# Giving out the steps of a windowed softmax one at a time, in a two-attention kernel whose instruction order comes from a planner

## The chip, the cores and the metric

One core of one Trainium2 chip. The metric is the device time of one execution in microseconds, median of several runs. Engines are named as the profile names them: PE (TensorE, matmuls; PEld are its weight loads), DVE (VectorE), ACT (ScalarE), POOL (GpSimd), SP (SyncE).

## The reference

Two attention layers over their own inputs, joined along the last axis. Both have 2048 positions, width 1024, 32 heads of 32. Layer A is dilated: each position sees 8 keys at distances 0, 2, ..., 14. Layer B sees the 256 latest keys.

```python
def _A_ref(x, wqkv, wo):
    qkv = (x @ wqkv) ...                      # q, k, v, each (1, 32, 2048, 32)
    off = jnp.arange(8) * 2
    idx = pos[:, None] - off[None, :]
    logits = jnp.einsum("bhsd,bhswd->bhsw", q, k[idx]) * Dh ** -0.5   # idx < 0 masked
    o = jnp.einsum("bhsw,bhswd->bhsd", softmax(logits), v[idx])
    return o.reshape(B, S, D) @ wo

def _B_ref(x, wqkv, wo):
    scores = q @ k.T * Dh ** -0.5             # masked to 0 <= i - j < 256
    return (softmax(scores) @ v).reshape(B, S, D) @ wo

return jnp.concatenate([A, B], axis=-1)
```

All is float32. The kernel reaches that precision on TensorE with pairs: a value is split into a high part and a rest, and three products of the pairs replace one.

## The kernel before, in words

**Units.** The work is cut into 8 units of 512 positions: units 0 to 3 are layer B, units 4 to 7 layer A. For layer A the even and the odd positions are laid out one after the other beforehand, so that a dilated window becomes a run of 8 neighbours. Each unit has 8 groups of 4 heads. For each group the projection of queries and keys is computed (`qk_items`, L616: 24 matmuls per weight tile), for several groups at once the values (`v_items`, L685), and one unit later the output projection (`o_items`, L749). A value part of four groups takes a new weight tile every 12 matmuls; such a part stands at the start of each unit.

**Splits.** Weights and inputs come in as float32 by loads that POOL issues (L182) into three buffers. `Stream.parts` splits them: a cast gives the high part, on ACT (L233) or DVE (L236), whichever the planner's books say is done sooner, and a subtraction on DVE gives the rest (L239), in pieces of 512 columns. `split_to` asks for a split; it is called where a matmul step is given out, mostly one tile ahead.

**Layer A's attention** (`window`). Scores of one group: 128 small matmuls into four banks (L822). Then, on a buffer `band` of 128 x 1152:
- four mask additions on DVE (L830);
- `top`: maximum (L840) and subtraction (L842) on DVE, then the exponential on ACT (L846);
- `total`: sum (L854), reciprocal (L856), product (L858) and two transposes of 32 x 32 blocks (L861, one for each half), all on DVE;
- `spread`, once for each half: eight copies on ACT (L870 and L873, four strips of two) that put the turned pieces in place along a diagonal of `wide`;
- values: small matmuls from `wide` and the values (L896), then the overlap of blocks is added and the result split (L994 to L1007) into `ot`, which the output projection reads.

**The planner.** The order on each engine is not the compiler's. While the program is built, an object `ck` of class `Clock` keeps books: `use` adds an operation's estimated time to an engine and returns when its result is seen, `defer(t, f)` calls `f` when the planned time of PE reaches `t`. The main loop picks, among four sequences (the projections `g`, scores `1`, values and second matmuls `2`, and `a`), the step that is ready first, gives out its matmuls, and calls what has fallen due in between. On the chip each engine then works through its instructions in the order in which they were given out; semaphores guard the data. Values are ready for the planner at `h["p"]`, which `spread` sets. Tables such as `PACE`, `HOLD` and `EDGES_V` shift these times by unit and group.

Of the kernel before, what the change touches and what calls it, by code (L numbers as in the profile page):

```python
# [9 lines left out]
AF = mybir.ActivationFunctionType  # L10
ALU = mybir.AluOpType
# [3 lines left out]
P = 128  # L15
# [19 lines left out]
PACE = ((0.4, 2.4, 0.1, 0.1, 0.4, -99, 4), (0.4, 1.8, 0.3, 0.1, 0.4, -99, 2), (0.1, 0.6, 0.3, 0.1, 0.0, -99, 2), (0.2, 2.4, 0.3, 0.1, 0.4, -99, 1), (6.0, 8.0, 0.5, 0.5, 1, 3), (2.0, 6.0, 1.5, 0.2, 1, 2), (4.0, 7.0, 0.5, 0.2, 1, 3), (4.0, 7.0, -0.5, 0.0, 1, 1))  # L35
# [7 lines left out]
HOLD = ((0, 1.2, 0, 0, 0, 0, 0, 0), (0, 0, 0, 0, 1.2, 0, 0, 0), (0.6, 0, 1.6, 0, 0, 0, 0, -0.4), (1.2, 0, 0, 0, 0, 0, 0, 1.2), (0, 0, 0, 0, 0, 0, 0, 0), (0, 0, 0, 0, 0, 0, 0, 0), (-0.4, 0, 0, 0, 0, 0, 0, 0), (0, 0, 0, 0, 0, 0, 0, 0))  # L43
# [7 lines left out]
class Clock:  # L51
# [6 lines left out]
    HOLD = dict(sp=0.63, act=0.35, pool=0.6)  # L58
    MOVE = dict(load=(2.12, 0.14), store=(0.64, 0.4), copy=(1.18, 0.56),
                halo_out=(0.4, 0.68), halo_in=(0.55, 0.6), halo_few=(0.28, 0.51),  # L60
                half=(1.0, 0.14), part=(0.33, 0.56))
# [96 lines left out]
class Stream:  # L158
# [68 lines left out]
    def parts(self, t, raw, t0, side):  # L227

        nc, ck = self.nc, self.ck
        n = raw.shape[1]  # L230
        bias = EARLY if side else self.light[self.split]
        if ck.ends("act", n / 1200 + 0.1, t0) <= ck.ends("dve", n / 1932 + 0.19, t0) + bias:
            nc.scalar.copy(t[:, 0, :], raw)  # L233
            r = ck.use("act", n / 1200 + 0.1, t0)
        else:
            nc.vector.tensor_copy(t[:, 0, :], raw)  # L236
            r = ck.use("dve", n / 1932 + 0.19, t0)
        for c in range(0, n, 512):
            nc.vector.tensor_tensor(t[:, 1, c:c + 512], raw[:, c:c + 512], t[:, 0, c:c + 512].bitcast(F32), op=ALU.subtract)  # L239
            end = ck.use("dve", 0.61, r, port=True)  # L240
        return end
# [19 lines left out]
def kernel(ctx, tc, xs, wqk, wv, wo, outs, units):  # L261


    nc = tc.nc
# [18 lines left out]
    ck = Clock()  # L283


    def parts_of(u):
        return VPARTS if len(V_AT[u]) == 3 else VPARTS_LATER
# [41 lines left out]
    for p in plan:  # L329
# [19 lines left out]
        else:  # L349
            u = p[1] - 1  # L350
# [8 lines left out]
    for key, i in where.items():  # L359
        u = min(key[1] + (key[0] == "o"), U - 1)  # L360
# [432 lines left out]
    def window(u, s):  # L793


        has_halo = units[u][3]
        buf = s % 2
        hg = u * NG + s
        vp, vc = vparts[parts_of(u)][s]
        v = vbufs[parts_of(u)][vp]  # L800

        def p96():
            return band[buf][:, :1536].rearrange("p (j b c) -> p j b c", j=4, b=4)

        def p16():
            return band[buf][:, :1536].rearrange("p (i c) -> p i c", c=96)[:, :, 24:]

        h = pairs[hg % 2] = {}

        def scores_ready():  # L810
            return latest(rs.empty(), done["stack"].get((u, s)),
                          latest(*[done["clear"].get(i) for i in range(2)]) if hg - 2 <= last_dense else
                          done["o"].get(hg - 2))

        def scores():
            qk = rows[hg]
            banks = [rs.take() for _ in range(4)]
            for b in range(4):
                for i in range(2):
                    for j in range(4):  # L820
                        c = P * b + 64 * i
                        nc.tensor.matmul(banks[j][0][64 * i:64 * i + 64, 72 * b:72 * b + 72],  # L822
                                         qk[32 * j:32 * j + 32, c:c + 64], qk[32 * j:32 * j + 32, S + c:S + c + 72],
                                         start=True, stop=True)
            seat_free(hg)

            def mask():
                m = cst["near"][:, 1:5] if has_halo else cst["near"][:, :4]
                for j in range(4):
                    nc.vector.tensor_tensor(p96()[:, j, :, 24:], banks[j][0][:, :288].rearrange("p (b c) -> p b c", b=4), m,  # L830
                                            op=ALU.add)
                    e = ck.use("dve", 0.37, ck.now)
                    rs.give(banks[j][1], e)
                ck.defer(e - 0.1, top)

            return mask

        def top():
            nm = small.tile([P, 16], F32, tag="nm", name="nm")
            nc.vector.tensor_reduce(nm, p16(), axis=mybir.AxisListType.X, op=ALU.max)  # L840
            ck.use("dve", 1.39, ck.now)
            nc.vector.tensor_tensor(p16(), p16(), nm[:, :, None].to_broadcast([P, 16, 72]), op=ALU.subtract)  # L842
            e = ck.use("dve", 1.39, ck.now, port=True)

            def expo():
                nc.scalar.activation(p16(), p16(), AF.Exp)  # L846
                e2 = ck.use("act", 1.07, e)
                ck.defer(e2 - 0.1, lambda: total(e2))

            ck.defer(e - 0.1, expo)  # L850

        def total(e):
            sm = small.tile([P, 16], F32, tag="sm", name="sm")
            nc.vector.tensor_reduce(sm, p16(), axis=mybir.AxisListType.X, op=ALU.add)  # L854
            ck.use("dve", 1.39, e)
            nc.vector.reciprocal(sm, sm)  # L856
            ck.use("dve", 0.285, ck.now)
            nc.vector.tensor_tensor(p16(), p16(), sm[:, :, None].to_broadcast([P, 16, 72]), op=ALU.mult)  # L858
            ck.use("dve", 1.39, ck.now, port=True)
            for i in range(2):  # L860
                nc.vector.transpose(turned[i], band[buf][:, 768 * i:768 * i + 768])  # L861
                e = ck.use("dve", 0.88, ck.now)
                ck.defer(e - 0.1, lambda i=i, e=e: spread(i, e))

        def spread(half, e):
            pieces = turned[half].rearrange("p (j b t c) -> p j b t c", j=2, b=4, t=3)
            diag = wide[buf][:, 2 * half:2 * half + 2].rearrange("p j (b c) -> p j b c", b=4)
            for i in range(4):
                r, c = 32 * i, 32 * i + 8
                nc.scalar.copy(diag[r:r + 32, :, :, c:c + 32], pieces[r:r + 32, :, :, 1 + i % 2, :])  # L870
                ck.use("act", 0.415, e)
                n, c = ((i - 1) * 32, c) if i else (96, 0)
                nc.scalar.copy(diag[n:n + 32, :, :, c:c + 8], pieces[r:r + 32, :, :, i % 2, :8])  # L873
                t = ck.use("act", 0.255, e)
            if half:
                h["p"] = t + PACE[u][3] + HOLD[u][s]

        def values_ready():
            if len(seats_x.free) < len(both):
                return None  # L880
            return latest(done["v"].get((u, vp)), *[x.get("p") for x in both], ro.when(),
                          rs.when() if alone else rs.empty())

        def values():
            own = ro if alone or s % 2 else rs
            h["o"], first_bank = own.take()
            h["o2"], bank = rs.take()
            halves = [h["o"], h["o2"]]
            blocks = [(-1, 1, 0, 8)] if has_halo else []
            blocks += [(b, i, P * b + 64 * i, min(72, S - P * b - 64 * i)) for b in range(4) for i in range(2)]  # L890
            seen = set()
            for b, i, q0, w in blocks:
                c = 136 * b + 8 + 64 * i if b >= 0 else 0
                r = slice(64 * i, 64 * i + 64)
                for j in range(4):
                    nc.tensor.matmul(halves[i][32 * j:32 * j + 32, q0:q0 + w],  # L896
                                     v[r, (4 * u + b) % 6, vc + 32 * j:vc + 32 * j + 32], wide[buf][r, j, c:c + w],
                                     start=(i, j) not in seen, stop=True, skip_group_check=True)
                    seen.add((i, j))

            return lambda: overlap(u, s, h, bank, own, first_bank, 0 if has_halo else 1)

        alone = s // 2 not in PAIRS[u]
        h["values"], both = values, [h] if alone else list(pairs)

        def two():
            ends = [x["values"]() for x in both]

            def after():
                for f in ends:  # L910
                    f()

            return after

        return [Item(scores_ready, scores, CW)], [Item(values_ready, two, C3 + len(both) * CP)] if alone or s % 2 else []
# [361 lines left out]
    while True:  # L1277
# [3 lines left out]
        for name, seq in seqs.items():  # L1281
# [3 lines left out]
            t = seq[pos[name]].ready()  # L1285
# [4 lines left out]
        if ck.later and (best is None or ck.later[0][0] < best[0]):  # L1290
            t = ck.later[0][0]
# [3 lines left out]
        t, name = best  # L1295
# [52 lines left out]
```

## Time and profile before

| | |
|---|---|
| median of 3 runs | 1779.6 us (1779.0 to 1781.2) |
| the profiled execution | 1781.06 us, span 1779.3 us |
| PE busy | 1766.2 us, 99% |
| PEld busy | 1474.0 us, 83% |
| DVE busy | 1260.9 us, 71% |
| ACT busy | 1048.8 us, 59% |
| granted TensorE clock, mean | 0.999 |
| mean DMA traffic | 145 GB/s |

A row of a group of instructions names line, engine, operation, what it writes and reads, and the count; then the busy time and the mean of one. A row of the timeline begins with the start and the duration in us; in square brackets stands how long the engine was idle just before, and what ended that. "Issue" is time in which an engine waited for nothing that the profile shows. PEclk is the clock granted to TensorE, 1.00 being all of it.

### The profile page before, as it was taken

The numbers are of one execution on the slowest core, as the hardware profiler recorded it, in microseconds if no ns is written. First come the engines' busy times: TensorE is split into PE (matmuls) and PEld (weight loads), VectorE is DVE, ScalarE is ACT, GpSimd is POOL, SyncE is SP. The second block draws the span as 40 slices with busy tenths as digits, with TensorE's granted clock in tenths as the row PEclk, the third lists the DMA queues.
The fourth block names the chain that finished last, engine by engine and source line by source line (L and its number), as shares of the span: only waits on it lengthen the run. The fifth ranks groups of instructions, "written<-read, shape, count | busy, mean of one in ns | idle before, by whom it ended". The sixth has DMA issues, their size and how long they took to land.

```text
span 1779.3 us, 39469 instructions
## 1 busy us (share of the span) xinstructions
PE 1766.2 (99%) x15210; PEld 1474.0 (83%) x15210; DVE 1260.9 (71%) x2690; ACT 1048.8 (59%) x2629; POOL 375.4 (21%) x829
## 2 busy tenths in 40 slices
PE   9999999999999999999999999999999999999999
PEld 7888888888888888888888888877888888888897
DVE  5678776677676779665766578776678676957873
ACT  5677766765776666676666455644455445534452
POOL 3322323224222212232233300110001100110000
PEclk9999999999999999999999999999999999999999
DMA  6656655647555556545554443433444443544432
GB/s 207 159 149 174 175 139 151 161 136 207 151 156 162 146 151 185 141 141 139 144 162 123 137 137 120 154 120 125 139 121 141 145 129 119 156 142 126 130 104 83
DMA packets 109723, 257.51 MB, mean 145 GB/s; under 512 B 14560, under 2 KB 29920, under 8 KB 109536
## 3 DMA queue, kind: packets, MB, share of 16 engines
q0 software_dynamic: 41760, 152.06, 28.5%
q1 hardware_dynamic: 58560, 86.15, 18.4%
q10 hardware_dynamic: 9216, 16.78, 2.5%
q8 instruction: 120, 1.97, 0.5%
q14 instruction: 67, 0.55, 0.1%
HBM read 164.63 MB, written 23.07 MB: 105 GB/s over the span
## 4 chain that ended last, share of the span: by engine, by line
PE 90%; DVE 3%; ACT 2%; DMA 2%; issue 2%; POOL 0%; SPq 0%; DVEq 0%; ACTq 0%; POOLq 0%
PE g L616 30%; PE g L749 16%; PE g L685 14%; PE x L616 6%; PE s L1121 6%; PE s L1037 5%; PE o L1186 3%; PE x L749 3%; PE x L685 2%; PE s L822 1%; PE x L1186 1%; DVE w L239 1%; PE s L896 1%; DMA raw<-wv 1%; DMA raw<-xs 1%
## 5 line engine op out<-in xcount | busy, mean ns | idle before, releaser
L616 PE MATMUL g<-x,w 128*128 128x512 f32 x2568 | 639.3, 392 | 0.6 <-ACT w L233 0.6
L616 PEld LDWEIGHTS g<-x,w 128*128 128x128 f32 x2568 | 475.4, 188 | 89.6 <-ACT w L233 1.0
L239 DVE TENSOR_TENSOR w<-raw,w 128x512 fp32r<-128x512 f32 x514 | 335.9, 695 | 42.8 <-ACT w L233 36.3
L1042 DVE CUSTOM_DVE_ANT_0 s<-s,mask_d 128x384 f32<-128x384 f32 (+2 forms) x512 | 262.7, 555 | 137.4 <-PE s L1037 136.2
L685 PE MATMUL g<-w,x 128*128 128x256 f32 (+1 forms) x1872 | 331.5, 320 | 0.7 <-DVE w L239 0.7
L1047 ACT ACTIVATE s<-s,nm 128x384 f32<-128x384 f32 (+2 forms) x512 | 274.1, 536 | 65.9 <-DVE nm L1042 64.7
L685 PEld LDWEIGHTS g<-w,x 128*128 128x128 f32 x1872 | 277.5, 191 | 24.5 <-DVE w L239 1.4
L749 PE MATMUL g<-ot,w 128*128 128x512 f32 x1200 | 294.5, 392 | 0.0
L749 PEld LDWEIGHTS g<-ot,w 128*128 128x128 f32 x1200 | 222.4, 188 | 43.4
L1106 POOL TENSOR_SCALAR_AFFINE_SELECT pbuf<-pbuf 128x128 f32<-128x128 f32 (+1 forms) x498 | 191.6, 412 | 202.5 <-ACT pbuf L1128 188.5
L1128 ACT ACTIVATE pbuf<-s 128x512 f32<-128x512 f32 (+1 forms) x368 | 188.9, 602 | 49.7 <-PE s L1121 48.1
L236 DVE CAST w<-raw 128x1024 fp32r<-128x1024 f32 x189 | 137.2, 726 | 77.9 <-PE g L616 27.3
L182 POOL DMA_DIRECT2D raw<-wqk x126 | 69.1, 549 | 505.0 <-DVE w L239 300.2
L1037 PE MATMUL s<-kst,qst 96*128 96x384 f32 (+2 forms) x512 | 141.1, 338 | 2.1 <-issue 1.0
L870 ACT COPY wide<-wide 32x256 f32<-32x256 f32 x256 | 103.4, 404 | 47.1 <-DVE wide L861 43.5
L1121 PE MATMUL s<-qst,kst 128*128 128x128 f32 (+2 forms) x704 | 126.1, 307 | 0.5 <-ACT pbuf L1128 0.3
L616 PE MATMUL x<-x,w 128*128 128x512 f32 x504 | 122.3, 393 | 0.0
L1121 PEld LDWEIGHTS s<-qst,kst 128*128 128x128 f32 x704 | 107.7, 189 | 15.8 <-ACT s L1047 1.7
L1037 PEld LDWEIGHTS s<-kst,qst 96*128 96x128 f32 x512 | 92.6, 189 | 22.6 <-ACT s L1047 3.1
L616 PEld LDWEIGHTS x<-x,w 128*128 128x128 f32 x504 | 93.3, 188 | 20.2
L1047 ACT ACTIVATION_READ_ACCUMULATOR s<-s,nm 128x1 f32 x512 | 105.9, 207 | 0.2
L182 POOL DMA_DIRECT2D raw<-wo x64 | 35.8, 559 | 322.8 <-DVE w L239 175.5
(114 smaller groups left out, 1907.5 us busy)
## 6 DMA issues: line engine op xcount, KB each, us to landing
raw<-wqk POOLq DMA_DIRECT2D x126, 512.0 KB, 4.0
raw<-wv POOLq DMA_DIRECT2D x72, 512.0 KB, 4.7
raw<-wo POOLq DMA_DIRECT2D x64, 512.0 KB, 4.1
qst<-nat SPq DMA_DIRECT2D x96, 256.0 KB, 4.1
kst<-nat SPq DMA_DIRECT2D x96, 256.0 KB, 5.2
raw<-xs POOLq DMA_DIRECT2D x28, 512.0 KB, 4.5
outs<-ost ACTq DMA_DIRECT2D x56, 256.0 KB, 2.5
kst<-halo SPq DMA_DIRECT2D x72, 128.0 KB, 2.8
```

The lines of the kernel that those rows point to most:

```text
L182: self.nc.gpsimd.dma_start(raw if len(ap.shape) == 2 else raw.rearrange("p (a b) -> p a b", a=2), ap)
L236: nc.vector.tensor_copy(t[:, 0, :], raw)
L239: nc.vector.tensor_tensor(t[:, 1, c:c + 512], raw[:, c:c + 512], t[:, 0, c:c + 512].bitcast(F32), op=ALU.subtract)
L616: nc.tensor.matmul(h["ps"], h["w"][:, a, k * P:(k + 1) * P], xt[u][k][:, b, :], start=(k == 0 and i == 0), stop=(k == NK - 1 and i == 2))
L685: nc.tensor.matmul(ps, xt[u][kw * g + k][:, a, p0:p0 + P], h["w"][g][:, c, k], start=(first and t == 0 and half == 0), stop=(last and t == 2),
L749: nc.tensor.matmul(h["ps"], w[:, a, c:c + P], ot[u, k][:, b, :], start=(k == 0 and i == 0), stop=(k == NK - 1 and i == 2))
L1037: nc.tensor.matmul(ps[:, :n], q[0:96, j, b * P:(b + 1) * P], kk[0:96, j, c0:c1], start=True, stop=True)
L1042: nc.vector.tensor_tensor_reduce(ps[:, :n], ps[:, :n], mask[:, cut:full], scale=-1.0, scalar=BIG, op0=ALU.add, op1=ALU.min, accum_out=nm)
L1047: nc.scalar.activation(ps[:, :n], ps[:, :n], AF.Exp, bias=nm, scale=-1.0, accum_out=sm)
L1106: nc.gpsimd.affine_select(w, w, pattern=[[0, m], [step, n]], compare_op=ALU.is_ge, fill=0.0, base=base, channel_multiplier=chan)
L1121: nc.tensor.matmul(ps[:, x:x + w], kk[:, j, 256 + kb * P:256 + (kb + 1) * P], q[:, j, q0:q0 + w], start=True, stop=True)
L1128: nc.scalar.activation(w, ps[:, :m * n].rearrange("p (j n) -> p j n", j=m), AF.Exp)
```

## The change

Before, `top` gives out maximum and subtraction together, `total` gives out five DVE instructions together, and `spread` eight ACT copies together. After the change each step is given out on its own, a little before the planner has the one before it done: maximum, then subtraction; sum with reciprocal, then product, then the first transpose, then the second; and the copies strip by strip, two at a time. Whatever is given out in between, splits of weights above all, then stands between them in the engine's order. The instructions themselves are the same. `h["p"]` is set when both halves have had their last strip.

```diff
         def top():
             nm = small.tile([P, 16], F32, tag="nm", name="nm")
             nc.vector.tensor_reduce(nm, p16(), axis=mybir.AxisListType.X, op=ALU.max)
-            ck.use("dve", 1.39, ck.now)
-            nc.vector.tensor_tensor(p16(), p16(), nm[:, :, None].to_broadcast([P, 16, 72]), op=ALU.subtract)
-            e = ck.use("dve", 1.39, ck.now, port=True)
-
-            def expo():
-                nc.scalar.activation(p16(), p16(), AF.Exp)
-                e2 = ck.use("act", 1.07, e)
-                ck.defer(e2 - 0.1, lambda: total(e2))
-
-            ck.defer(e - 0.1, expo)
+            e1 = ck.use("dve", 1.39, ck.now)
+
+            def less():
+                nc.vector.tensor_tensor(p16(), p16(), nm[:, :, None].to_broadcast([P, 16, 72]), op=ALU.subtract)
+                e = ck.use("dve", 1.39, ck.now, port=True)
+
+                def expo():
+                    nc.scalar.activation(p16(), p16(), AF.Exp)
+                    e2 = ck.use("act", 1.07, e)
+                    ck.defer(e2 - 0.1, lambda: total(e2))
+
+                ck.defer(e - 0.1, expo)
+
+            ck.defer(e1 - 0.15, less)
 
         def total(e):
             sm = small.tile([P, 16], F32, tag="sm", name="sm")
             nc.vector.tensor_reduce(sm, p16(), axis=mybir.AxisListType.X, op=ALU.add)
             ck.use("dve", 1.39, e)
             nc.vector.reciprocal(sm, sm)
-            ck.use("dve", 0.285, ck.now)
-            nc.vector.tensor_tensor(p16(), p16(), sm[:, :, None].to_broadcast([P, 16, 72]), op=ALU.mult)
-            ck.use("dve", 1.39, ck.now, port=True)
-            for i in range(2):
+            r = ck.use("dve", 0.285, ck.now)
+
+            def parts():
+                nc.vector.tensor_tensor(p16(), p16(), sm[:, :, None].to_broadcast([P, 16, 72]), op=ALU.mult)
+                ck.defer(ck.use("dve", 1.39, ck.now, port=True) - 0.15, lambda: turn(0))
+
+            def turn(i):
                 nc.vector.transpose(turned[i], band[buf][:, 768 * i:768 * i + 768])
                 e = ck.use("dve", 0.88, ck.now)
-                ck.defer(e - 0.1, lambda i=i, e=e: spread(i, e))
+                ck.defer(e - 0.1, lambda: spread(i, e))
+                if not i:
+                    ck.defer(e - 0.15, lambda: turn(1))
+
+            ck.defer(r - 0.15, parts)
 
         def spread(half, e):
...
-            for i in range(4):
+
+            def strip(i):
                 r, c = 32 * i, 32 * i + 8
                 nc.scalar.copy(diag[r:r + 32, :, :, c:c + 32], pieces[r:r + 32, :, :, 1 + i % 2, :])
                 ck.use("act", 0.415, e)
                 n, c = ((i - 1) * 32, c) if i else (96, 0)
                 nc.scalar.copy(diag[n:n + 32, :, :, c:c + 8], pieces[r:r + 32, :, :, i % 2, :8])
                 t = ck.use("act", 0.255, e)
-            if half:
-                h["p"] = t + PACE[u][3] + HOLD[u][s]
+                if i < 3:
+                    ck.defer(t - 0.15, lambda: strip(i + 1))
+                else:
+                    h["strips"] = h.get("strips", 0) + 1
+                    if h["strips"] == 2:
+                        h["p"] = t + PACE[u][3] + HOLD[u][s]
+
+            strip(0)
```

## The prediction

> **What bounds the kernel now.** I read the page first, then the busy time by stages, then who waits for whom on TensorE, and last the order of instructions round each wait.
>
> ```profile
> span 1779.3 us, 39469 instructions
> PE 1766.2 (99%) x15210; PEld 1474.0 (83%) x15210; DVE 1260.9 (71%) x2690; ACT 1048.8 (59%) x2629; POOL 375.4 (21%) x829
> PE 90%; DVE 3%; ACT 2%; DMA 2%; issue 2%; POOL 0%; SPq 0%; DVEq 0%; ACTq 0%; POOLq 0%
> ```
>
> TensorE is busy for 1766.2 of 1779.3 us and carries 90% of the chain that ended last. An edit that moves no matmul can give back only what TensorE loses to waiting. Only layer A's softmax (its first step is L840) is edited, so nothing before 1023.8 us can move:
>
> ```profile
> L840 DVE TENSOR_REDUCE nm<-band x32: 1310/1351/1355, 1023.8 to 1729.0; 128x16 f32<-128x1152 f32 x32
> ```
>
> The row has the count, the durations in ns, and the first and last start. The waits of TensorE from 960 us to the end, with total, number and longest:
>
> ```profile
> PE x L685 <- DVE w L239: 1.6, 1, 1.6
> PE s L896 <- issue: 1.0, 1, 1.0
> PE s L822 <- issue: 0.8, 2, 0.6
> PE g L685 <- DVE w L239: 0.7, 2, 0.4
> ```
>
> These four rows are the whole list: 4.1 us. L685 is the value projection, L239 the second half of a split of weights. So 1.6 + 0.7 = 2.3 us are waits for splits, three of them; the other 1.8 us ("issue") wait for nothing that the trace names. No split is late anywhere else. The three are the starts of the second, third and fourth unit of layer A, where a four-group value part takes a new weight tile every 12 matmuls. The longest, on TensorE, VectorE and ScalarE in order of time (start, duration, idle before):
>
> ```profile
> 1357.71 0.84 PE L685 MATMUL x<-w,x 128*128 128x512 f32 x3
> 1360.43 0.39 PE L685 MATMUL x<-w,x 128*128 128x512 f32 x1
> 1362.40 0.73 PE L685 MATMUL x<-w,x 128*128 128x512 f32 x2 [1.58 <-DVE w L239]
> ...
> 1355.91 0.45 DVE L1007 TENSOR_TENSOR ot<-o,ot 128x288 fp32r<-128x288 f32 x1
> 1356.28 1.34 DVE L854 TENSOR_REDUCE sm<-band 128x16 f32<-128x1152 f32 x1
> 1357.65 0.25 DVE L856 RECIPROCAL sm<-sm 128x16 f32<-128x16 f32 x1
> 1357.94 1.36 DVE L858 TENSOR_TENSOR band<-band,sm 128x1152 f32<-128x1152 f32 x1
> 1359.33 1.84 DVE L861 STREAM_TRANSPOSE wide<-band 128x768 f32<-128x768 f32 x2
> 1361.10 1.25 DVE L239 TENSOR_TENSOR w<-raw,w 128x512 fp32r<-128x512 f32 x2
> ...
> 1355.73 1.06 ACT L233 CAST w<-raw 128x1024 fp32r<-128x1024 f32 x1
> ```
>
> The cast of that tile is done at 1355.73 + 1.06 = 1356.79, but VectorE comes to its second half at 1361.10, since sum, reciprocal, product and both transposes stand ahead of it, 1356.28 to 1361.17, 4.89 us. That block is what `total` gives out at once. The other two places:
>
> ```profile
> 1169.37 2.91 PE L685 MATMUL g<-w,x 128*128 128x512 f32 x7 [0.26 <-DVE w L239]
> 1555.14 0.73 PE L685 MATMUL g<-w,x 128*128 128x512 f32 x2 [0.43 <-DVE w L239]
> ...
> 1166.31 1.84 DVE L861 STREAM_TRANSPOSE wide<-band 128x768 f32<-128x768 f32 x2
> 1168.07 1.25 DVE L239 TENSOR_TENSOR w<-raw,w 128x512 fp32r<-128x512 f32 x2
> 1552.07 1.84 DVE L861 STREAM_TRANSPOSE wide<-band 128x768 f32<-128x768 f32 x2
> 1553.83 1.25 DVE L239 TENSOR_TENSOR w<-raw,w 128x512 fp32r<-128x512 f32 x2
> ```
>
> The same picture: both transposes, then the split, then TensorE.
>
> **The change part by part.** No instruction is added or removed; only the order on VectorE and ScalarE moves, and with it the planner's idea of when values (L896) can go.
>
> *VectorE steps one at a time.* A value part asks for its next tile at the first matmul of the current one. For the longest wait that is at 1357.71. The product's deferral falls due 0.035 us before the planner has the reciprocal done, at the trace's 1357.90. If the request comes first, the split runs 1357.9 to 1359.2, ahead of the need at 1360.43. If the product comes first, the split follows it at 1359.34 and ends at 1360.6, 0.2 us late. So of 1.58 us between 0 and 0.3 us stay. The two small waits need the split earlier by 0.26 and 0.43 us, less than one transpose (1.84 us for two), so they go whole. Gain 2.3 - 0.3 = 2.0 us. Its bounds: 0, if the planner asks too late, and 2.3.
>
> *What the softmax pays.* At each gap a split may come in, 1.25 us, or 0.69 us more with its cast on VectorE. Two per group make its end later by up to 2 x 1.94 = 3.9 us. What is queued behind are the strips (L870, L873) and then values on TensorE. The planner places values after the strips, and until then TensorE has matmuls of the projections; that cover hides it everywhere but in the last group, costed next. I take nothing, with the rival below as the other end.
>
> *The last group.* Nothing is left to cover it but the first columns of the output projection:
>
> ```profile
> 1737.73 1.84 DVE L861 STREAM_TRANSPOSE wide<-band 128x768 f32<-128x768 f32 x2
> 1739.49 0.39 DVE L236 CAST x<-raw 128x512 fp32r<-128x512 f32 x1
> ...
> 1743.10 0.69 DVE L239 TENSOR_TENSOR x<-raw,x 128x512 fp32r<-128x512 f32 x1
> ...
> 1746.33 0.46 DVE L1007 TENSOR_TENSOR ot<-o,ot 128x288 fp32r<-128x288 f32 x1
> ...
> 1750.85 0.84 PE L749 MATMUL g<-ot,w 128*128 128x512 f32 x3
> ```
>
> Its result is ready at 1746.79 and first needed at 1750.85: 4.06 us of cover. Four casts and four subtractions (eight rows, 1739.49 to 1743.79, 4.30 us) could all slip ahead of the transposes and would then cost 4.30 - 4.06 = 0.24 us; two columns of the output projection ask for them in turn, so probably only the first half does, inside the cover. Taken: 0, with 0.24 us as the upper end.
>
> *ScalarE strips in eights.* Casts and bank evacuations can now come between them. TensorE waits for neither in the list, so a gain is excluded unless it brings a split forward, which is counted. The loss is that of the softmax's end, above.
>
> *The clock.* In the first place the granted clock falls:
>
> ```profile
> core 0: us, PE busy (x) PEld busy (x) DVE busy (x) ACT busy (x) POOL busy (x), PEclk, DMA share, GB/s
> 1135.00:1140.00 5.00, 5.00 (x44) 5.00 (x43) 5.00 (x11) 1.37 (x4) 1.28 (x3) 1.00 0.59 188
> 1165.00:1170.00 5.00, 3.91 (x75) 2.68 (x74) 4.96 (x8) 2.59 (x9) 0.12 (x1) 0.99 0.33 106
> 1170.00:1175.00 5.00, 5.00 (x16) 3.73 (x14) 3.49 (x5) 4.36 (x11) 0.43 (x1) 0.67 0.36 105
> ```
>
> 5 x (1 - 0.67) = 1.65 us are lost after 5.00 - 3.91 = 1.09 us of idling, of which only 0.26 us are the split's; the other 0.84 us ("issue") stay. So I take nothing for the clock and keep 1.65 us as the lower end. The Trainium skill ("TensorE: Matmul & The Clock Gate", What's actually happening) has the clock halved after a whole idle window of about 3.4 us; the trace does not agree, 1.09 us spread over such a stretch was enough here. By that rule gaps of this size would move no clock, and the sum would be the same as the one taken, without the lower end.
>
> The sum, against the profiled execution: 1781.06 us (span 1779.3 and 1.8 around it) less 2.0 is 1779.1. The profiled execution is 1.5 us above the median of the runs, 1779.6, and the same 2.0 us from there gives 1777.6 us.
>
> **The rivals.** *Faster: the other gaps go too.* If the earlier split leaves the first place without the dip (1.65 us) and the 1.0 us gap at L896 does not recur, 1777.6 - 1.65 - 1.0 = 1774.9; with L822's 0.8 and the last 0.3 it would be 1773.8. For it: the dip needs a sum of idling, and part of it goes. Against: the "issue" gaps are nothing that this change touches.
>
> *Slower: softmax held behind splits that are not ready.* VectorE takes its queue in order. Across layer A it has idled at a split whose cast was late, as the list of all waits shows, and values follow the strips closely:
>
> ```profile
> DVE w L239 <- ACT w L233: 33.8, 23, 3.4
> ...
> 1348.33 0.24 ACT L873 COPY wide<-wide 32x64 f32<-32x64 f32 x1
> ...
> 1349.25 0.21 PE L896 MATMUL s<-wide,vbuf 64*32 64x8 f32 x4
> ```
>
> A hold lasts 33.8 / 23 = 1.47 us; the strips end at 1348.57 and values start 0.68 us later. A hold that the planner did not foresee, put inside the softmax, makes TensorE stop at L896 for 1.47 - 0.68 = 0.8 us. It would show at the starts of units, where VectorE has no gaps (5.00 of 5.00 us at 1135 to 1140): eight groups make 6.4 us, 1777.6 + 6.4 = 1784.0. It decides from seven groups on (5.6 us, the 2.0 gained and 3.6 on top). For it: every gap of the softmax is now open to such a split, and the margin is small. Against: the planner books the casts too, so only its errors count. The Trainium skill (the same page, Architectural detail) calls VectorE's and ScalarE's queues strict first in, first out; the 33.8 us agree, and by that rule no later softmax step can pass the split.
>
> *No effect: the freed split is not given out earlier, or waits for its data.* Then the waits change their name and the time is 1779.6. Against it: the cast above was done 4.3 us before VectorE came to it. For it: the tiles come in by loads that take as long as the block,
>
> ```profile
> raw<-wv POOLq DMA_DIRECT2D x72, 512.0 KB, 4.7
> ```
>
> 4.7 us from issue to landing against a 4.89 us block.
>
> **How the numbers follow.** A measurement of this kernel can tell about 0.2%, 3.6 us, from no change: under 1776.0 is faster, over 1783.2 slower. The forecast has 0.38 (1777.6, its own range 1776.0 to 1779.0), no effect 0.09 (1779.6), the other gaps 0.24 (1774.9), the held softmax 0.29 (1784.0). So faster 0.24, same 0.38 + 0.09 = 0.47, slower 0.29. The likeliest case gives 1777.6. The range runs from the lowest bound, 1773.8, to the held softmax at eight groups, 1784.0; about half of that rival lies above it, and with the ends of the others nearly 2 in 10 are outside.
>
> **What would show it.** Right: the two rows of L685 waiting for L239 are gone or under 0.3 us; between L854 and the second transpose at the starts of units stands an L239; values start later than before, without idle time at L896. The last group's L1007 still ends before the first matmul that reads it. Wrong: new rows of L896 or L822 waiting for ScalarE's strips (the held softmax); L685 waiting for a cast or a load instead (no effect); more stretches with the clock under 1.00; or a gap of TensorE ahead of the last columns.

## The result, and the profile after

The changed kernel takes 1777.49 us (median of 22 runs, 1775.35 to 1779.84), the kernel before 1780.39 us beside it (22 runs, 1778.2 to 1783.35): a ratio of 0.9982, 95% interval 0.9976 to 0.9989, or 2.9 us less. The profiled execution took 1779.02 us. Its page:

```profile
span 1777.3 us, 39486 instructions
PE 1764.8 (99%) x15210; PEld 1472.3 (83%) x15210; DVE 1243.5 (70%) x2666; ACT 1065.4 (60%) x2653; POOL 372.8 (21%) x829
PE 94%; ACT 2%; DMA 1%; DVE 1%; issue 1%; POOL 1%; SPq 0%; POOLq 0%; ACTq 0%; DVEq 0%
```

VectorE's share of the chain that ended last fell from 3% to 1%, TensorE's rose from 90% to 94%. VectorE is busy 17 us less and ScalarE 17 us more: 24 instructions went from VectorE to ScalarE, 15 of them casts of splits (L233: 102 before, 117 now). The planner chooses the engine of a cast by its books, so more than the order moved. Opening the strips is not the main reason: with the VectorE steps alone, below, there are 113 already. The waits of TensorE from 960 us on:

```profile
PE s L914 <- ACT wide L885: 1.7, 2, 1.4
PE g L749 <- DVE ot L1025: 0.4, 1, 0.4
PE s L914 <- issue: 0.3, 1, 0.3
```

(Lines moved: values are L914 instead of L896, strips L882 and L885, product L864, transposes L868.) No wait of L685 for a split is left. The start of the third unit of layer A, where the longest had been, on VectorE:

```profile
1354.03 1.35 DVE L858 TENSOR_REDUCE sm<-band 128x16 f32<-128x1152 f32 x1
...
1355.82 1.36 DVE L864 TENSOR_TENSOR band<-band,sm 128x1152 f32<-128x1152 f32 x1
1357.81 1.30 DVE L239 TENSOR_TENSOR w<-raw,w 128x512 fp32r<-128x512 f32 x2 [0.64 <-ACT w L233]
1359.02 0.97 DVE L868 STREAM_TRANSPOSE wide<-band 128x768 f32<-128x768 f32 x1
1359.92 0.20 DVE L1014 TENSOR_TENSOR o<-o,band 128x64 f32<-128x64 f32 x1
1360.03 0.70 DVE L236 CAST w<-raw 128x1024 fp32r<-128x1024 f32 x1
1360.77 1.29 DVE L239 TENSOR_TENSOR w<-raw,w 128x512 fp32r<-128x512 f32 x2
1361.98 0.97 DVE L868 STREAM_TRANSPOSE wide<-band 128x768 f32<-128x768 f32 x1
```

One split stands ahead of the first transpose, another between the two. The clock dip at the start of the second unit is gone as well:

```profile
1165.00:1170.00 5.00, 5.00 (x24) 4.14 (x23) 4.97 (x7) 2.59 (x8) 1.11 (x2) 1.00 0.36 105
1170.00:1175.00 5.00, 5.00 (x24) 4.14 (x23) 2.86 (x4) 3.39 (x9) 0.00 (x0) 1.00 0.39 105
```

In its place values wait for strips. The timeline of ScalarE, VectorE and TensorE:

```profile
1092.02 0.40 ACT L882 COPY wide<-wide 32x256 f32<-32x256 f32 x1 [2.25 <-DVE wide L868]
...
1096.38 0.40 ACT L882 COPY wide<-wide 32x256 f32<-32x256 f32 x1 [0.36 <-DVE wide L868]
...
1091.01 0.97 DVE L868 STREAM_TRANSPOSE wide<-band 128x768 f32<-128x768 f32 x1
1095.37 0.98 DVE L868 STREAM_TRANSPOSE wide<-band 128x768 f32<-128x768 f32 x1 [3.38 <-ACT wide L885]
...
1099.11 0.25 PE L914 MATMUL s<-wide,vbuf 64*32 64x72 f32 x2 [1.44 <-ACT wide L885]
```

A strip waits for a transpose, the next transpose waits for a strip, and values wait for the last strip. The code says why. `turned` has two tiles, one for each half, and every group uses both. Given out at once, a group's strips were through before the next group's transposes came. One at a time, the strips of two groups interleave, and VectorE and ScalarE take turns waiting. Moreover ten strips of three groups (32, 34 and 38) are given out after the next group's transpose into the same tile and put that group's pieces in place of their own. So the changed kernel, as it stands, no longer does the work of the kernel before and is not one to use. A kernel below restores each strip's own pieces.

### The profile page after: what moved, and what is told of

Read it like the earlier page. It is cut to its first block, busy times and chain, and to the rows that moved or that the text cites. A ratio compares the mean times of both kernels' runs of the same rounds, so it can differ in the third digit from the quotient of the medians.

```text
span 1777.3 us, 39486 instructions
## 1 busy us (share of the span) xinstructions
PE 1764.8 (99%) x15210; PEld 1472.3 (83%) x15210; DVE 1243.5 (70%) x2666; ACT 1065.4 (60%) x2653; POOL 372.8 (21%) x829
## 4 chain that ended last, share of the span: by engine, by line
PE 94%; ACT 2%; DMA 1%; DVE 1%; issue 1%; POOL 1%; SPq 0%; POOLq 0%; ACTq 0%; DVEq 0%
PE g L616 31%; PE g L749 16%; PE g L685 15%; PE x L616 7%; PE s L1139 6%; PE s L1055 5%; PE x L685 3%; PE o L1204 3%; PE x L749 3%; PE s L822 2%; PE x L1204 1%; PE s L914 1%; DMA raw<-wv 1%; PE o L914 1%; ACT s L1065 0%
## 5 line engine op out<-in xcount | busy, mean ns | idle before, releaser
L616 PE MATMUL g<-x,w 128*128 128x512 f32 x2568 | 640.1, 392 | 1.1 <-ACT w L233 0.8
L616 PEld LDWEIGHTS g<-x,w 128*128 128x128 f32 x2568 | 475.1, 188 | 90.7 <-ACT w L233 1.3
L685 PE MATMUL g<-w,x 128*128 128x256 f32 (+1 forms) x1872 | 329.8, 319 | 0.3 <-DVE w L239 0.2
L685 PEld LDWEIGHTS g<-w,x 128*128 128x128 f32 x1872 | 276.2, 190 | 23.5 <-DVE w L239 0.6
L749 PE MATMUL g<-ot,w 128*128 128x512 f32 x1200 | 294.4, 392 | 0.4 <-DVE ot L1025 0.4
L749 PEld LDWEIGHTS g<-ot,w 128*128 128x128 f32 x1200 | 222.4, 188 | 44.1 <-DVE ot L1025 0.8
L236 DVE CAST w<-raw 128x1024 fp32r<-128x1024 f32 x179 | 130.2, 727 | 65.5 <-PE g L616 24.2
L882 ACT COPY wide<-wide 32x256 f32<-32x256 f32 x256 | 103.3, 404 | 37.3 <-DVE wide L868 33.1
L616 PE MATMUL x<-x,w 128*128 128x512 f32 x504 | 121.6, 393 | 0.0
L616 PEld LDWEIGHTS x<-x,w 128*128 128x128 f32 x504 | 93.5, 188 | 20.0
```

The costliest lines, as they stand in the source:

```text
L616: nc.tensor.matmul(h["ps"], h["w"][:, a, k * P:(k + 1) * P], xt[u][k][:, b, :], start=(k == 0 and i == 0), stop=(k == NK - 1 and i == 2))
L685: nc.tensor.matmul(ps, xt[u][kw * g + k][:, a, p0:p0 + P], h["w"][g][:, c, k], start=(first and t == 0 and half == 0), stop=(last and t == 2),
L749: nc.tensor.matmul(h["ps"], w[:, a, c:c + P], ot[u, k][:, b, :], start=(k == 0 and i == 0), stop=(k == NK - 1 and i == 2))
```

## The experiments

All switch the same places. `step` either defers, as the change does, or calls at once, as before; with both conditions false the order on each engine is that of the kernel before.

```diff
+        one_dve, one_act = ..., ...
+        def step(alone_, t, f):
+            if alone_:
+                ck.defer(t, f)
+            else:
+                f()
...
-            ck.defer(e1 - 0.15, less)
+            step(one_dve, e1 - 0.15, less)
...
-            ck.defer(r - 0.15, parts)
+            step(one_dve, r - 0.15, parts)
...
-                    ck.defer(t - 0.15, lambda: strip(i + 1))
+                    step(one_act, t - 0.15, lambda: strip(i + 1))
```

Line numbers move again in these kernels: values are L921 and, with the guard below, L927; the two copies of a strip L889 and L892, with the guard L893 and L896; transposes L875 and L879.

The theory: the gain is that of splits which pass the VectorE block at the starts of units. The rivals: it comes from the strips; it is spread over all groups; any new order does it, since chance gaps and the dip then fall otherwise.

| kernel | ratio | 95% interval | median us | TensorE waits from 960 us on, us | mean granted clock |
|---|---|---|---|---|---|
| changed | 0.9982 | 0.9976 to 0.9989 | 1777.49 | 2.4 | 1.000 |
| VectorE steps alone | 0.9964 | 0.9950 to 0.9978 | 1774.39 | 0.2 | 1.000 |
| strips alone | 1.0082 | 1.0069 to 1.0095 | 1794.70 | 11.1 | 0.995 |
| last groups alone | 1.0009 | 1.0000 to 1.0018 | 1782.16 | 4.7 | 0.998 |
| all but last groups | 1.0048 | 1.0035 to 1.0060 | 1788.51 | 10.5 | 0.997 |
| VectorE steps, guarded | 0.9987 | 0.9978 to 0.9996 | 1779.18 | 2.4 | 0.999 |
| whole change, guarded | 0.9970 | 0.9959 to 0.9981 | 1775.63 | 0.8 | 1.000 |
| six groups, VectorE steps | 0.9967 | 0.9955 to 0.9980 | 1775.39 | 0.3 | 1.000 |
| values 0.3 us later, no step open | 1.0005 | 0.9996 to 1.0013 | 1781.89 | 3.9 | 0.999 |
| six groups, from the sum on | 0.9966 | 0.9954 to 0.9979 | 1774.91 | 0.7 | 1.000 |
| six groups, steps and strips | 0.9964 | 0.9951 to 0.9977 | 1774.38 | none | 1.000 |

Each ratio is against the kernel before, measured beside it (medians of 1780.4 to 1780.8 us). The waits and the clock are those of one profiled execution of each kernel. Before, the waits were 4.1 us and the mean clock 0.999.

**VectorE steps alone** (`one_dve, one_act = True, False`).

> The VectorE steps (maximum, subtraction, sum, product, two transposes) are given out one at a time, the ScalarE strips in eights as before. Theory, splits past the VectorE block at the starts of units: the three waits of L685 for L239 (2.3 us) are gone or under 0.3 us, the gain is that of the whole change, about 2.9 us, ratio 0.998. Rival, the strips: the gain comes from ScalarE's work between the copies, so this one is at 1.000 of the kernel before. Rival, any new order does it (the clock dip of 1.65 us and the gaps put down to issue, 1.8 us, fall away by chance): 0.998 as well, but with L685 waits left.

The whole list of TensorE's waits:

```profile
PE g L685 <- DVE w L239: 0.2, 1, 0.2
```

The L685 waits are gone, as the theory had it, and the gain, 0.36%, is twice that of the whole change, though the intervals overlap at 0.9976 to 0.9978. The strips go out in eights here, so opening them cannot be its cause. All eight strips of group 38 go after group 39's transposes here and take its pieces.

**Strips alone** (`False, True`).

> Only the ScalarE strips are given out one at a time, the VectorE block at once as before. Theory, splits past the VectorE block: the three L685 waits stay at about 2.3 us, ratio 0.9995 to 1.0005. Rival, the strips: 0.998. Rival, any new order: 0.998 or whatever the chance gaps give, with the L685 waits in place.

The largest of TensorE's waits:

```profile
PE s L921 <- ACT wide L892: 6.1, 2, 3.9
PE x L749 <- DVE w L239: 3.3, 1, 3.3
PE x L685 <- DVE nat L523: 1.1, 1, 1.1
```

The stretch after the wait of L749, by windows (busy times, then the granted clock, the DMA share and GB/s):

```profile
1585.00:1590.00 5.00, 5.00 (x12) 3.94 (x13) 4.30 (x7) 3.71 (x12) 1.39 (x3) 0.50 0.47 119
```

All three expectations fell short: 14 us slower. Half of the waits are values waiting for strips (L892), the rest splits and what stands behind a closed VectorE block, and after the gap the clock is down, 0.50 over 5 us; over layer A 8.5 us are lost to the clock in three places (summed over windows of 5 us), against 1.7 us in the kernel before. One strip each of groups 32 (both halves), 34 and 38 takes the next group's pieces. The rival that the strips bring the gain is refuted; opened alone, they cost. Of the three waits of L685 one is left, at the start of the third unit, under another name. It is put down to the clearing of a small tile (L523), but a split behind two transposes ends only 0.02 us before that:

```profile
1365.59 1.25 DVE L239 TENSOR_TENSOR w<-raw,w 128x512 fp32r<-128x512 f32 x2
...
1366.79 0.07 DVE L523 MEMSET nat<- 128x8 f32 x1
...
1366.89 0.73 PE L685 MATMUL x<-w,x 128*128 128x512 f32 x2 [1.10 <-DVE nat L523]
```

The other two are gone although the block is closed. At the start of the second unit the values' wait for strips, 3.9 us, stands in their place, and at the fourth the late split is that for L749, behind the transposes of the next block.

**Last groups alone** (`s == NG - 1 and u < U - 1` for both) **and all but these** (`not (...)`).

> All steps one at a time, but only for the last group of units 4, 5 and 6, three groups of 32: by the trace it is their softmax that stood before the late splits. Theory, starts of units: the L685 waits go, 2.3 us, and with them perhaps the clock dip, ratio 0.998 to 0.9988. Rival, the gain is spread over all groups: 3/32 of it, 1.000. Rival, any new order: between.

> The reverse: all steps one at a time in 29 groups, at once in the last group of units 4, 5 and 6. Theory, starts of units: the L685 waits for L239 stay near 2.3 us in three places, ratio about 1.000. Rival, spread over all groups: 0.998. Rival, any new order: 0.998 or so with the L685 waits in place.

With the last groups alone, TensorE's whole list but for 0.3 us:

```profile
PE x L749 <- DVE w L239: 2.4, 1, 2.4
PE g L616 <- ACT w L233: 2.0, 1, 2.0
```

What stood before the longer one, on the timeline of VectorE and TensorE:

```profile
1572.61 1.84 DVE L875 STREAM_TRANSPOSE wide<-band 128x768 f32<-128x768 f32 x2
1574.37 1.25 DVE L239 TENSOR_TENSOR w<-raw,w 128x512 fp32r<-128x512 f32 x2
...
1575.08 1.17 PE L749 MATMUL x<-ot,w 128*128 128x512 f32 x3 [2.40 <-DVE w L239]
```

The L685 waits went, as expected; the time did not, and my 0.998 to 0.9988 was wrong. The late split moved to the next block, that of the next unit's first group: transposes, then the split, then L749. The other wait, 2.0 us, is for a late cast on ScalarE, and after each of the two gaps the clock dips, 0.66 over 5 us. With all but the last groups open, the waits of L685 stayed and grew:

```profile
PE g L685 <- DVE w L239: 4.6, 2, 2.3
PE x L685 <- ACT w L233: 1.7, 1, 1.7
PE g L616 <- DVE w L239: 1.6, 1, 1.6
```

The waits of L685 stand at the starts of the second, third and fourth unit. The ratio, 1.0048, is worse than all three expectations. So the last groups are needed and not enough. Fifteen strips of groups 32, 34, 46 and 47 take another group's pieces in this one; with the last groups alone none does.

**With a guard.** From here on, in every kernel that opens a step, a transpose waits, in the planner, until the group before has given out its last strip from the same tile; each strip then takes its own pieces.

```diff
             def turn(i):
+                if i in held:
+                    held[i].append(lambda: turn(i))
+                    return
+                held[i] = []
...
                 else:
+                    for f in held.pop(half):
+                        ck.defer(t - 0.1, f)
                     h["strips"] = h.get("strips", 0) + 1
```

VectorE steps alone, with it:

> VectorE steps one at a time, strips in eights, and in addition a transpose is not given out before the last strip of the group before has read the same half of `turned`, which both groups of a pair share. Without this, in the kernel with the VectorE steps alone, the eight strips of one group (38) read what the transposes of the next (39) had written; with it each strip reads its own group's pieces. Theory, splits past the VectorE block: the guard touches one pair, far from the starts of units, so the gain stays, ratio 0.996 to 0.997, and no wait of L685 over 0.3 us. Rival, the gain came from the strips that went out of turn: ratio 0.998 or more, with new waits of values for strips near 1090 us.

The theory's ratio was missed: 0.9987. No wait of L685 is over 0.3 us, as it had it, but there is a new wait, for a cast and not for strips, and not near 1090 us but at 1182 us. TensorE's longest:

```profile
PE g L616 <- ACT w L233: 1.4, 1, 1.4
```

ScalarE's timeline there:

```profile
1181.14 0.24 ACT L896 COPY wide<-wide 32x64 f32<-32x64 f32 x1
...
1182.32 1.04 ACT L233 CAST w<-raw 128x1024 fp32r<-128x1024 f32 x1
```

The cast that L616 needs stands behind strips given out at once and three short instructions that evacuate banks. This is the block on ScalarE that does what the one on VectorE did. The unguarded kernel did not meet it. The expectation also had the place of the guarded pair wrong. Groups 38 and 39 are the last two of unit 4, so the pair is not far from a start of a unit but at one. The transposes of the two groups, in the kernel with the VectorE steps alone and no guard:

```profile
1166.47 3.86 DVE L875 STREAM_TRANSPOSE wide<-band 128x768 f32<-128x768 f32 x4
```

and with it:

```profile
1168.45 1.83 DVE L879 STREAM_TRANSPOSE wide<-band 128x768 f32<-128x768 f32 x2
...
1174.81 0.97 DVE L879 STREAM_TRANSPOSE wide<-band 128x768 f32<-128x768 f32 x1
1176.05 0.98 DVE L879 STREAM_TRANSPOSE wide<-band 128x768 f32<-128x768 f32 x1 [0.26 <-ACT wide L896]
```

The whole change, guarded:

> The whole change with the same guard. In the change without it ten strips of three groups (32, 34, 38) read the next group's pieces; here none does. Theory: strips one at a time cost time, because the strips of two groups get in each other's way (values wait 1.7 us for strips in the changed kernel); the guard ends the mixing, so the wait at 1097 us goes and the ratio is 0.9965 to 0.998. Rival, the strips cost time because casts and copies between them make the softmax late: the waits of values for strips stay, 0.998 to 0.9995.

The wait at 1097 us is gone; what is left:

```profile
PE g L749 <- DVE ot L1038: 0.4, 1, 0.4
PE s L927 <- ACT wide L896: 0.2, 1, 0.2
PE s L927 <- issue: 0.2, 1, 0.2
```

0.9970 against 0.9982: the medians are 1.9 us apart and the wait was 1.4 us, though the intervals overlap. By the waits, the mixing of two groups was what the strips cost, not the strips as such; by the time alone that is not shown.

**Six groups** (`one_dve` only for the last group of units 4 to 6 and the first of units 5 to 7, strips in eights, guard).

> VectorE steps one at a time only in the last group of units 4 to 6 and the first group of units 5 to 7, six groups of 32; strips in eights; the guard as well. With the last groups alone the three L685 waits went, but at 1572 us a split for L749 came 2.4 us late behind the block of the next unit's first group. Theory, starts of units: both blocks there have to be open, and these six give all of the gain, ratio 0.996 to 0.997. Rival, the gain needs the other 26 groups: 0.9985 to 1.001.

TensorE's list:

```profile
PE s L927 <- issue: 0.3, 1, 0.3
```

As expected: six groups of 32 give the whole gain. The rival that it is spread over all groups is refuted. In the kernels that open six groups no transpose ever has to be held, so the guard has no part in this.

**A new order alone** (in the kernel before, `h["p"] = t + PACE[u][3] + HOLD[u][s] + 0.3`).

> The kernel before with the planned time of layer A's values 0.3 us later and nothing else: every order after 1050 us may change, no step is opened. Theory, splits past the block: the L685 waits for L239 stay near 2.3 us in three places and the ratio is 0.9985 to 1.004, not a gain of 0.36%. Rival, any new order does it: the ratio may be 0.9965 as well.

```profile
PE g L685 <- DVE w L239: 1.4, 2, 1.2
PE x L685 <- DVE w L239: 1.2, 1, 1.2
```

1.4 + 1.2 = 2.6 us in three places, and no gain. This new order does not remove the waits. Another one may: in the kernel with the strips alone two of the three are gone although the block is closed, but there the time was lost at other places. What no kernel here shows is a gain from a new order alone.

**Six groups, only from the sum on; six groups, strips too.**

> As the six-group kernel (last group of units 4 to 6, first of units 5 to 7, strips in eights, guard), but only sum, product and the two transposes are given out one at a time; maximum and subtraction stay together. Theory: the block that stood before the late splits is that of the sum, 4.9 us long, against 2.7 us for maximum and subtraction; opening it alone gives the whole gain, ratio 0.9965 to 0.9975, no L685 wait over 0.3 us. Rival: at the starts of units VectorE has no gap, so the 2.7 us block in front of a split matters as well and part of the waits stays, 0.998 to 0.9995.

> As the six-group kernel, with the strips of these six groups one at a time too. Theory: at the starts of units a cast can now pass the strips (in the kernel with guarded VectorE steps a cast stood behind eight copies at 1182 us and L616 waited 1.4 us), but the six-group kernel has no such wait left, so nothing is gained: ratio 0.9962 to 0.9972, the same within the interval. Rival, the strips cost by themselves: 0.998 or more, values waiting for strips.

TensorE's list for the first; that of the second is empty:

```profile
PE s L927 <- issue: 0.7, 1, 0.7
```

Both as expected. The block that mattered is that of the sum, 4.9 us. With all six groups wholly open and the guard, TensorE waits for nothing in layer A, and at 1774.38 us, ratio 0.9964, this is the fastest of the kernels here in which each strip takes its own pieces; the other two six-group kernels are the same within their intervals.

## Why the prediction was right

The forecast was 1777.6 us and the measured median is 1777.49. Its first step holds: the three waits for splits (2.3 us) are gone, and the experiments show that they go where a split can pass the block of the sum, in the groups at the starts of units. That the two figures agree to 0.1 us is luck. The sum started 0.8 us too low, from the median of three runs, 1779.6 us; over 22 it is 1780.39. And it took off 0.9 us too little, 2.0 us instead of 2.9. Terms that I had set to zero were not zero and offset each other in part: most of the gaps put down to "issue" went, and the strips cost something.

In the two profiled executions the waits of TensorE went from 4.1 to 2.4 us: 2.3 us less for splits, 1.5 us less of "issue", 1.7 us more for strips and 0.4 us more for the output of the last group but one. Layer A's attention begins with the mask additions of its first group, before and after:

```profile
1022.18 1.55 DVE L830 TENSOR_TENSOR band<-s,near 128x288 f32<-128x288 f32 x4 [3.55 <-PE s L822]
```

```profile
1024.17 1.19 DVE L830 TENSOR_TENSOR band<-s,near 128x288 f32<-128x288 f32 x3 [3.55 <-PE s L822]
```

From there to the end of the span it took 1779.3 - 1022.2 = 757.1 us and takes 1777.3 - 1024.2 = 753.1 us, 4.0 us less: 1.7 us of waits, 1.65 us of clock, and about 0.6 us that stand on neither list. What comes before that row is the same work in both, and it took 2.0 us longer in the second execution, so single executions are no measure of so small a change.

- *The clock.* I took nothing, on the ground that only 0.26 of 1.09 us of idling were the split's. In the profiled execution the dip (1.65 us) went. But it is not what parts the medians. Of 47 executions of the kernel before that ran beside the experiments, 36 have a mean granted clock of 1.000, where a loss of 1.65 us in 1779 would give 0.999; their median is 1780.7 us. The changed kernel has 1.000 in 20 of 22, with a median of 1777.2 us. Of the 1.8 us put down to "issue" 0.3 us are left; whether the earlier splits did that was not tried. This is the rival "the other gaps go too", and the kernels with under 1 us of waits left, at 1774.4 to 1775.6 us, lie about its 1774.9.
- *The strips.* I took nothing: matmuls of the projections were to cover a later end of the softmax everywhere but in the last group. At 1099 us they did not. A wait of values for strips is the sign of the rival of the held softmax, and the prediction named it a sign of being wrong; it came with 1.7 us in all, 1.4 us of it at one place, instead of 0.8 us at each of eight groups. The cause was another than the rival's. It was not a cast that was late but the two tiles of `turned`, which the groups share and which I had not looked at.
- *The last group.* The cover held. One pair of subtractions came between the transposes, the result was ready at 1745.43 and first needed at 1748.82:

```profile
1737.37 1.25 DVE L239 TENSOR_TENSOR x<-raw,x 128x512 fp32r<-128x512 f32 x2
...
1744.97 0.46 DVE L1025 TENSOR_TENSOR ot<-o,ot 128x288 fp32r<-128x288 f32 x1
...
1748.82 0.84 PE L749 MATMUL g<-ot,w 128*128 128x512 f32 x3
...
1732.88 0.73 PE L749 MATMUL g<-ot,w 128*128 128x512 f32 x2 [0.39 <-DVE ot L1025]
```

The last row is a wait that I had missed: the group before it, in the first column, 0.4 us.

Two things are not settled. With 1.7 us of waits gone the medians are 2.9 us apart, and in the kernels that open six groups 4.1 us of waits became 0.7 us or less and the time fell by 5.4 to 6.4 us; where the rest comes from is not shown. And it is open why the guard on the VectorE steps, which moves only the pair of groups 38 and 39, ends in an order in which the cast at 1182 us is late; the planner's choices between were not followed one by one.

## What to carry to other kernels

Where engines take their queues in order, the length of what is given out at once is a priority: 5 us of work without a deadline, given out together ahead of 2 us with one, is a stall. Look for the few places where TensorE's margin is near zero and open the blocks there; here six groups of 32 gave all of it. Before opening a sequence, list the tiles that its steps share with the next round: what was safe because it went out whole may mix, wait in turns, and read the wrong round's data.

## What the hardware showed

A gap of TensorE can cost more than its length. In the kernel before, 1.09 us of idling within 5 us were followed by 5 us at a mean granted clock of 0.67; in the kernel with the strips alone 0.50 was granted over 5 us after its gap of 3.3 us. Yet a single gap of 1.58 us at 1360 us in the kernel before brought no dip:

```profile
1300.00:1400.00 100.00, 98.42 (x1030) 83.60 (x1030) 74.31 (x114) 48.34 (x113) 12.54 (x22) 1.00 0.45 135
```

The columns are the busy time of the engines, then the clock, 1.00, over these 100 us. So near this length the length alone does not tell which gap brings a dip. In layer A of the profiled executions here, all seven gaps of 2.0 to 3.9 us were followed by one, and of five single gaps of 1.4 to 1.6 us only one was, that of 1.4 us at 1182 us in the kernel with the guarded VectorE steps. Each dip cost about 1.7 us, two of the three in the kernel with the strips alone twice that. Nor does the order of instructions fix it: the kernel before shows the lower mean clock in only 11 of 47 executions.
